# Spectral mixer with channel MLP, four layers: outer products added over two banks at once, weights' parts made beside the inner products

## The chip, the cores and the metric

The kernel runs on one core of a Trainium2 chip. Its engines run beside each other, each with its own queue in a fixed order: TensorE (PE in the profile, with its weight loads as PEld), VectorE (DVE), ScalarE (ACT), GpSimd (POOL) and SyncE (SP, whose queue issues all DMAs here). They wait for each other by semaphores. The metric is the device time of one execution in microseconds (us); the median of several runs counts.

## The reference

A token matrix x of 2048 x 576 goes through two pairs of layers, all in float32:

```python
x = x + _A_ref(_layernorm(x, axis=-1), A_dft_seq_re, A_dft_seq_im, A_dft_hid_re, A_dft_hid_im)
x = x + _B_ref(_layernorm(x, axis=-1), B_w1, B_b1, B_w2, B_b2)
x = x + _A_ref(_layernorm(x, axis=-1), A_dft_seq_re, A_dft_seq_im, A_dft_hid_re, A_dft_hid_im)
x = x + _B_ref(_layernorm(x, axis=-1), B_w1, B_b1, B_w2, B_b2)
```

`_A_ref` is the real part of a Fourier transform along the hidden dimension and along the sequence, as products with given cosine and sine matrices. `_B_ref` is a layer norm of its own, then `gelu(y @ w1 + b1) @ w2 + b2`, with w1 of 576 x 4608 and w2 of 4608 x 576.

## The kernel before

**Precision.** Each float32 operand of a product is split in two parts: the high part is the value rounded to TensorE's float32r format (a ScalarE copy), the low part is the rest (a subtraction). A product is then three matmuls, high x high, high x low and low x high (`PASSES`, L44). For w1 a block row of 288 values is held as two blocks of 128 and a third block in which the last 32 rows stand three times, so that high and low parts of the last rows share one matmul of 96 rows.

**Seven products for eight.** Each large product of 2 x 2 blocks is made by seven block products of sums and differences (Winograd's form of Strassen's scheme). They are numbered 1 to 7. `ORDER` (L33) is their order in the inner products, `OUTER` (L43) that in the outer products: 1, 6, 5, 3 and then 7, 4, 2.

**Stages.** For each layer pair: the sequence transform (`Sequence.run`), then for two halves of 1024 tokens the hidden transform (`hidden`) and the MLP (`mlp`). The four MLP stages are called passes 1 to 4 here. Pass 1 (layer 0, half 0; `first` is true) also makes the w2 parts and the rest of the w1 parts, and stores both to DRAM for the passes after it.

**One MLP pass.** F is cut in 18 pieces q; two of them, 2g and 2g + 1, make a group g (NG = 9). The loop at L1118 runs over g = 0 to 9. For g from 1 to 8 it does: the inner products of q = 2g (the *even inner phase*, seven products of seven matmuls with 512 columns), the outer products 1, 6, 5, 3 of group g - 1 (*outer phase A*, four products of 24 matmuls with 288 columns), the inner products of q = 2g + 1 (*odd inner phase*) and the outer products 7, 4, 2 of group g - 1 (*outer phase B*). g = 0 has inner phases alone, g = 9 outer phases alone.

*Inner phase* (`inner`, L976). Even q uses PSUM banks 0 to 3, odd q banks 4 to 7. Products 1 and 2 share the first of the four banks, 6 has the second, 5 and 3 share the third, 7 and 4 the fourth: the later product adds to what the earlier left, so it waits until that has been read. After product 1 ScalarE copies the bank (L1013), after 6 VectorE adds (L1015), after 5 ScalarE copies (L1019) and GpSimd adds the copy and product 1 and 6's sum (L1020), after 7 VectorE adds that (L1022), and product 4 may then write. Gelu follows in place (L986).

*Steps* (`step`, L1041). The result of an inner phase is turned into the seven left operands H of the outer products in eight steps: ScalarE copies the high part (L1047), VectorE or, from step 4 on, GpSimd makes the low part of the step before (L1051), and VectorE makes the next sum or difference from step 1 to 4. Steps are queued in `tasks`; `work(1)` puts one of them on the engines' queues, after each inner product and in each *slot* of an outer phase.

*Outer phase* (`outer`, L1070). A slot is half a product: 12 matmuls into the two banks of a pair `pp[2 * side + jj]`, six for each bank. After the matmuls of a slot come, in this order on the queues: a step, the second weights' work that is due (`advance`), a `tick`, and the addition of both banks to the accumulator in SBUF, one VectorE instruction for each bank (L1094, L1096). The slot after next writes the same pair. Phase A uses banks 4 to 7, phase B banks 0 to 3.

**Weights' parts.** `weights` (L244) is a generator for the w1 parts, 126 in number (18 pieces of seven). One pump of it takes the part begun before, makes its low part with two VectorE subtractions (L264, L265), stores it (L266), lets GpSimd make the next sum or difference of raw blocks where one is due, loads a raw block, and begins the next part with one ScalarE copy (L281). `tick(share)` pumps it in `share` of four calls: in three of four steps of the first sequence transform (L623), in one of four inner products and outer slots of pass 1 (L1031, L1088). `make` (L927) lists for a group of w2 when each of its seven parts is begun (`hi`, a ScalarE copy) and finished (`lo`, a VectorE subtraction and a store), when GpSimd makes sums of raw blocks, and when raw blocks of the next group are loaded. The first number of an entry is its due time: 0 to 6 are the products of the even inner phase, 7 to 14 the slots of phase A, 15 to 21 the odd inner phase, 22 to 27 phase B. The weights' loads for the inner and outer products (`load_w`) go over the same SyncE queue as these stores and loads. Buffers for w1 parts are five in pass 1 and seven in the others; those for w2 parts three.

## Time and profile before

| what | value |
|---|---|
| median of 3 runs | 2779.91 us |
| the runs | 2789.28, 2779.21, 2779.91 us |
| span of the profiled execution | 2780.2 us (no time of its own is listed for it) |
| mean granted TensorE clock | 0.996 |
| first matmul of the first sequence transform | 11.3 us |
| pass 1, from its first full inner phase to the end of its last | 472.7 to 875.3 us |
| pass 2, the same stretch | 1013.5 to 1379.1 us |
| pass 3, the same stretch | 1882.2 to 2247.9 us |
| pass 4, the same stretch | 2376.3 to 2741.9 us |

A row of busy time by stretches gives: the stretch, its length, then busy time and number of instructions of PE, PEld, DVE, ACT and POOL, the granted clock, the share of DMA time and GB/s. A row of the order of time gives: start, duration, engine, line, operation, output and inputs, number of instructions merged into it, and in brackets the idle time before it with what ended it. A row of the groups gives: line, engine, operation, shape and number, then busy time, mean duration in ns and idle time before. A row of waits gives: who waited for whom, us in total, times, longest.

### The profile page before, as it was taken

Reading aid. Unit: us, or ns where it says so; the run is one execution under the profiler, and the core shown is the slowest. Engines: PE = TensorE matmul, PEld = TensorE weight load, DVE = VectorE, ACT = ScalarE, POOL = GpSimd, SP = SyncE. Lnnn points to the kernel's source line nnn. Section 1 sums busy time; section 2 is a strip of 40 time slices with the busy share of each in tenths; the row PEclk is TensorE's granted clock in tenths of the full one; section 3 lists DMA queues with packets and bytes.
Section 4 is the critical chain, followed back from the end, with each engine's and each line's share of the span. In section 5 each row is a group of like instructions: output and inputs, shape, how many; then the busy total and the mean of one; then the engine's idle time right before and its main releaser. Section 6 shows DMA issues by size and latency. Waiting matters only on the chain. (4 is left out here: it accounts for less than half of the span.)

```text
span 2780.2 us, 46515 instructions
## 1 busy us (share of the span) xinstructions
PE 2687.9 (97%) x17596; PEld 2511.9 (90%) x17596; DVE 1793.9 (65%) x3179; ACT 1113.4 (40%) x1827; POOL 898.4 (32%) x836
## 2 busy tenths in 40 slices
PE   7999999999998999999989999999999999999999
PEld 7999998778887989898989999998888889988888
DVE  8888965777776555555577666555555564655555
ACT  6444434544443343333344333334333333433332
POOL 5232234544544442222241000043222234322223
PEclk9999999999999999999999999999999999999999
DMA  5676764777775646666563333426666664666664
GB/s 202 231 230 217 236 212 136 265 263 249 266 269 193 208 134 193 193 191 189 160 235 111 125 118 124 162 90 205 191 193 192 193 213 135 184 192 192 189 197 157
DMA packets 205551, 530.54 MB, mean 191 GB/s; under 512 B 21632, under 2 KB 56448, under 8 KB 205184
## 3 DMA queue, kind: packets, MB, share of 16 engines
q1 hardware_dynamic: 205328, 527.57, 59.2%
q8 instruction: 140, 2.29, 0.3%
q14 instruction: 83, 0.68, 0.1%
HBM read 420.73 MB, written 109.41 MB: 191 GB/s over the span
## 5 line engine op out<-in xcount | busy, mean ns | idle before, releaser
L198 PE MATMUL bank<-R 128*128 128x288 f32 (+2 forms) x16972 | 2629.2, 315 | 79.6 <-DVE A L188 42.6
L198 PEld LDWEIGHTS bank<-R 128*128 128x128 f32 x16972 | 2445.9, 189 | 253.8 <-DVE A L188 55.9
L188 DVE TENSOR_TENSOR A<-bank,A 128x288 f32<-128x288 f32 (+1 forms) x1260 | 561.6, 477 | 399.1 <-PE bank L198 356.6
L188 POOL TENSOR_TENSOR A<-A 128x512 f32<-128x512 f32 (+4 forms) x178 | 229.0, 1290 | 998.3 <-ACT A L1019 410.2
L191 POOL TENSOR_TENSOR R<-A,R 128x512 fp32r<-128x512 f32 x288 | 372.8, 1305 | 535.1 <-ACT R L1047 532.2
L191 DVE TENSOR_TENSOR R<-A,R 128x1024 fp32r<-128x1024 f32 (+6 forms) x575 | 475.6, 840 | 41.2 <-ACT R L544 25.0
L188 DVE TENSOR_TENSOR bank<-bank,A 128x512 f32<-128x512 f32 (+1 forms) x228 | 153.0, 671 | 360.1 <-POOL A L188 262.8
L1047 ACT ACTIVATE R<-A 128x512 fp32r<-128x512 f32 x288 | 175.6, 628 | 287.9 <-PE bank L198 256.6
L986 ACT ACTIVATE bank<-bank,b1t 128x512 f32<-128x512 f32 (+1 forms) x224 | 144.9, 647 | 359.6 <-DVE bank L188 198.1
L191 DVE TENSOR_TENSOR R<-bank,R 128x512 fp32r<-128x512 f32 (+4 forms) x408 | 251.4, 635 | 50.9 <-ACT R L194 44.5
L544 ACT ACTIVATE R<-A 128x1024 fp32r<-128x1024 f32 x196 | 204.1, 1054 | 147.4 <-DVE A L191 119.5
L191 POOL TENSOR_TENSOR A<-A 128x288 f32<-128x288 f32 (+2 forms) x170 | 211.1, 1251 | 151.5 <-DVE R L191 91.6
L191 DVE TENSOR_TENSOR A<-A 128x1024 f32<-128x1024 f32 (+2 forms) x116 | 130.5, 1130 | 4.2 <-ACT A L238 1.2
L1047 ACT ACTIVATE R<-bank 128x512 fp32r<-128x512 f32 x216 | 120.8, 596 | 29.3 <-PE bank L198 29.3
L194 ACT ACTIVATE R<-bank 128x512 fp32r<-128x512 f32 (+2 forms) x160 | 74.0, 514 | 145.8 <-PE bank L741 90.9
L1013 ACT ACTIVATE A<-bank 128x512 f32<-128x512 f32 (+1 forms) x76 | 43.7, 575 | 180.2 <-PE bank L198 171.0
L191 DVE TENSOR_TENSOR A<-bank,A 128x512 f32<-128x512 f32 x144 | 98.0, 681 | 0.1
L238 ACT ACTIVATE A<-A,moments 128x576 f32<-128x576 f32 x64 | 54.0, 868 | 107.6 <-POOL moments L221 75.8
L281 ACT ACTIVATE R<-A 128x384 fp32r<-128x384 f32 x126 | 65.1, 516 | 18.1 <-DMA w_parts<-R 7.4
L1019 ACT ACTIVATE A<-bank 128x512 f32<-128x512 f32 (+1 forms) x76 | 43.7, 575 | 62.4 <-PE bank L198 62.4
L584 DVE SCALAR_TENSOR_TENSOR A<-A 128x288 f32<-128x288 f32 x28 | 16.0, 571 | 77.4 <-POOL A L188 77.4
L219 POOL TENSOR_TENSOR moments<-moments,power 128x1 f32<-128x1 f32 x32 | 17.6, 551 | 144.1 <-DVE moments L216 144.1
(48 smaller groups left out, 670.9 us busy)
## 6 DMA issues: line engine op xcount, KB each, us to landing
R<-w_parts SPq DMA_DIRECT2D x504, 320.0 KB, 3.4
R<-w_parts SPq DMA_DIRECT2D x189, 576.0 KB, 3.7
A<-in_cs SPq DMA_DIRECT2D x112, 512.0 KB, 4.2
w_parts<-R SPq DMA_DIRECT2D x126, 320.0 KB, 3.3
w_parts<-R SPq DMA_DIRECT2D x63, 576.0 KB, 3.2
uv_mid<-A SPq DMA_DIRECT2D x32, 576.0 KB, 2.8
A<-in_w SPq DMA_DIRECT2D x72, 192.0 KB, 3.5
R<-dh_mid SPq DMA_DIRECT2D x36, 288.0 KB, 5.7
```

What stands on the lines that cost most here:

```text
L188: engine.tensor_tensor(dst, a, b, op=op)
L191: engine.tensor_tensor(dst, a, b, op=OP.subtract)
L194: nc.scalar.activation(hi, src, AF.Copy)
L198: nc.tensor.matmul(o, a, b, start=start, stop=stop, skip_group_check=True)
L219: nc.gpsimd.tensor_tensor(mv[:, 3:4], mv[:, 2:3], power[:, 0:1], op=OP.pow)
L238: nc.scalar.activation(dst, src, AF.Identity, bias=mv[:, 4:5], scale=mv[:, 3:4])
L281: nc.scalar.activation(at(n)[:, :3 * P], steps[n % 7][1], AF.Copy)
L544: nc.scalar.activation(self.cells[t, i](2, NP, P)[:, 0], self.source(t, i), AF.Copy)
L986: nc.scalar.activation(dst, src, AF.Gelu_apprx_tanh, bias=bias(f))
L1013: nc.scalar.activation(up, o, AF.Copy)
L1019: nc.scalar.activation(tp, o, AF.Copy)
L1047: nc.scalar.activation(H[q, k](2, TC)[:, 0], src, AF.Copy)
```

## The change

Five things are changed.

1. The eight PSUM banks are one tile, and a pair `pp[i]` is a view of two neighbouring banks. The addition of an outer slot, and that of a tile in the hidden transform, is one VectorE instruction over both banks (2 x 288) where there were two of 288.
2. The parts of w1 are laid out anew: low, high, shared, high, low. One VectorE subtraction of 3 x 128 makes all the low parts; for that the third block of the high part holds zeros outside rows 32 to 63 (a ScalarE instruction of its own with a scale for each partition, the new column `middle`), so that a part is begun with two ScalarE instructions. The raw blocks are laid out to fit, and so are the operands of the inner products.
3. `tick` is called in inner products alone, with a share of two of four, and its calls are spread evenly. In pass 1 that is seven pumps a group, as before.
4. `make` has new due times for all groups but the last: parts 1, 5 and 6 in the even inner phase, part 3 in phase A, parts 7, 4 and 2 in the odd inner phase. Both sums that follow part 1 are made at once.
5. Of three slots in an outer phase the third carries no step, except in the last two groups of outer products; the steps left over go to the next inner phase.

```diff
-    banks = [psum.tile([P, 512], F32, name=f"bank{i}") for i in range(8)]
-    pp = [(banks[2 * i], banks[2 * i + 1]) for i in range(4)]
+    bank = psum.tile([P, 8, 512], F32, name="bank")
+    banks = [bank[:, i] for i in range(8)]
+    pp = [bank[:, 2 * i:2 * i + 2] for i in range(4)]
...
+    middle = const.tile([P, 1], F32, name="middle")
...
+        def cut(a):
+            return a.rearrange("p (k f) -> p k f", f=P)
+
+        def high(n):
+            src, t = cut(steps[n % 7][1]), cut(at(n))
+            nc.scalar.activation(t[:, 1:4:2], src[:, 0:3:2], AF.Copy)
+            nc.scalar.activation(t[:, 2], src[:, 1], AF.Identity, bias=power[:, 2:3], scale=middle)
...
-            t = at(n)
-            sub(nc.vector, t[:, 3 * P:], src[:, :2 * P], t[:, :2 * P].bitcast(F32))
-            sub(nc.vector, t[32:64, 2 * P:3 * P], src[32:64, 2 * P:], t[32:64, 2 * P:3 * P].bitcast(F32))
-            dma(w1s[q, i - 1], t.bitcast(F32))
+            t = cut(at(n))
+            sub(nc.vector, t[:, 0:5:2], cut(src), t[:, 1:4].bitcast(F32))
+            dma(w1s[q, i - 1], at(n).bitcast(F32))
...
-                nc.scalar.activation(at(n)[:, :3 * P], steps[n % 7][1], AF.Copy)
+                high(n)
...
-        if ticks[0] % 4 < share:
+        if ticks[0] * share % 4 < share:
...
-            for e in range(2):
-                add(nc.vector, tile_x[:, e], o[e][:, :DH], tile_x[:, e])
+            add(nc.vector, tile_x, o[:, :, :DH], tile_x)
...
-            return [(1, lambda: hi(1, b11)),
-                    (2, lambda: (lo(1, b11), sub(pool, b11, b12, b11))), (3, lambda: sub(pool, x, b22, b11)),
-                    (5, lambda: hi(6, x)), (6, lambda: lo(6, x)),
-                    (7, lambda: hi(5, b11)), (8, lambda: (lo(5, b11), load_raw(g + 1, 0), sub(pool, x, b21, x))),
-                    (9, lambda: hi(3, b22)),
-                    (10, lambda: (lo(3, b22), sub(pool, b12, b22, b12), load_raw(g + 1, 2))),
-                    (12, lambda: hi(7, b12)), (13, lambda: (lo(7, b12), load_raw(g + 1, 1))),
-                    (14, lambda: hi(4, x)), (15, lambda: lo(4, x)),
-                    (16, lambda: hi(2, b21)), (17, lambda: (lo(2, b21), load_raw(g + 1, 3)))]
+            one = [lambda: hi(1, b11), lambda: (lo(1, b11), sub(pool, b11, b12, b11), sub(pool, x, b22, b11))]
+            six = [lambda: hi(6, x), lambda: (lo(6, x), sub(pool, x, b21, x))]
+            five = [lambda: hi(5, b11), lambda: (lo(5, b11), load_raw(g + 1, 0))]
+            three = [lambda: hi(3, b22), lambda: (lo(3, b22), sub(pool, b12, b22, b12), load_raw(g + 1, 2))]
+            seven = [lambda: hi(7, b12), lambda: (lo(7, b12), load_raw(g + 1, 1))]
+            four = [lambda: hi(4, x), lambda: lo(4, x)]
+            two = [lambda: hi(2, b21), lambda: (lo(2, b21), load_raw(g + 1, 3))]
+            if g == NG - 1:
+                return list(zip((1, 2, 5, 6, 7, 8, 9, 10, 12, 13, 14, 15, 16, 17),
+                                one + six + five + three + seven + four + two))
+            return list(zip((0, 1, 2, 3, 4, 5, 9, 10, 15, 16, 17, 18, 19, 20),
+                            one + five + six + three + seven + four + two))
...
-                    todo += [(w[:, k], yi[:, k]), (w[:, k], yi[:, 3 + k]), (w[:, 3 + k], yi[:, k])]
+                    todo += [(w[:, 1 + 2 * k], yi[:, k]), (w[:, 1 + 2 * k], yi[:, 3 + k]), (w[:, 4 * k], yi[:, k])]
...
-                    tick(1)
+                    tick(2)
...
+        slot = [0]
+
         def outer(g, i, side):
...
-                work(1)
+                work(slot[0] % 3 < 2 or g >= last - 1)
+                slot[0] += 1
                 advance()
-                tick(1)
...
-                for j in range(2):
-                    if i == 6 and g == 0:
-                        nc.vector.tensor_copy(to[:, j], o[j][:, :DH])
-                    else:
-                        add(nc.vector, to[:, j], o[j][:, :DH], to[:, j])
+                if i == 6 and g == 0:
+                    nc.vector.tensor_copy(to, o[:, :, :DH])
+                else:
+                    add(nc.vector, to, o[:, :, :DH], to)
...
+                    slot[0] = 0
                     for i in OUTER[f]:
                         outer(g - 1, i, 1 - f)
...
+    nc.gpsimd.memset(middle, 0.0)
+    nc.gpsimd.memset(middle[32:64], 1.0)
...
-                w1[:, :, at, k] = block[k * P:(k + 1) * P].transpose(1, 0, 2)
+                w1[:, :, at, 2 * k] = block[k * P:(k + 1) * P].transpose(1, 0, 2)
             for r in range(3):
-                w1[:, 32 * r:32 * r + 32, at, 2] = block[2 * P:].transpose(1, 0, 2)
+                w1[:, 32 * r:32 * r + 32, at, 1] = block[2 * P:].transpose(1, 0, 2)
```

On the engines' queues of the program that results, TensorE has the same instructions in the same order. In groups 2 to 7 of pass 1, GpSimd's queue now has in the even inner phase, in this order: two low parts of steps, the two sums that follow w2 part 1, a w1 sum, two low parts of steps, and then the sum after product 5 (L1020). VectorE has 662 instructions fewer, ScalarE 126 more.

More of the change, by code (lines that the diff above doesn't have):

```diff
@@ L739, in turn @@
             for k in range(KH):
-                at = (*a, *b)[k // 4][:, k % 4 * P:(k % 4 + 1) * P]
+                at = (a, b)[k // 8][:, k // 4 % 2, k % 4 * P:(k % 4 + 1) * P]
                 nc.tensor.transpose(at, v[:, k], ident)
-            for k0, k1, at in ((0, 4, a[0]), (4, 8, a[1]), (8, 9, b[0][:, 0:P])):
+            for k0, k1, at in ((0, 4, a[:, 0]), (4, 8, a[:, 1]), (8, 9, b[:, 0, 0:P])):
                 split(o[:, 0, k0:k1], o[:, 1, k0:k1], at.rearrange("p (k t) -> p k t", t=P))
@@ L806, in turn_y @@
                     o = space()
-                ob = o[i0 // 2 % 2]
+                ob = o[:, i0 // 2 % 2]
                 ni = min(2, 7 - i0)
@@ L817, in turn_y @@
             for i0 in (0, 4):
-                ob = o[i0 // 4]
+                ob = o[:, i0 // 4]
                 ni = min(4, 7 - i0)
@@ L846, in hidden @@
                     for e in range(2):
-                        mm(o[e][:, :DH], u(2, KH, P)[:, a, k], h.dd[k][b](2, DH)[:, e],
+                        mm(o[:, e, :DH], u(2, KH, P)[:, a, k], h.dd[k][b](2, DH)[:, e],
                            k == 0 and m == 0, k == KH - 1 and m == 2)
@@ L1078, in outer @@
                         for n, (a, b) in enumerate(PASSES):
-                            mm(o[j][:, :DH], h[:, a, at], w[:, b], i in (1, 5, 7, 2) and f == 0 and n == 0,
+                            mm(o[:, j, :DH], h[:, a, at], w[:, b], i in (1, 5, 7, 2) and f == 0 and n == 0,
                                i in (6, 3, 2, 4) and f == 1 and n == 2)
```

## The prediction

> **What bounds the kernel now.** I read the page first, then busy time by stretches, then the order of time in one group of the MLP.

> ```profile
> span 2780.2 us, 46515 instructions
> PE 2687.9 (97%) x17596; PEld 2511.9 (90%) x17596; DVE 1793.9 (65%) x3179; ACT 1113.4 (40%) x1827; POOL 898.4 (32%) x836
> ...
> 210.00:280.00 70.00, 70.00 (x532) 70.00 (x531) 62.03 (x83) 33.12 (x51) 19.73 (x12) 1.00 0.70 227
> ```

> TensorE sets the time: at 97% only some 90 us are idle, though a wait hidden in the modelled ends of its matmuls comes on top. The third row (busy time of PE, PEld, DVE, ACT, POOL; then clock and DMA) is a stretch of the sequence transform in which the first weights' parts are made: PE never pauses, so cheaper work on other engines gains nothing there. The MLP is where time can be had. The next rows cut one group (g = 3) of pass 1 (layer 0, half 0, which also makes the weights' parts) and one of pass 2, each into even inner phase, outer phase A (products 1, 6, 5, 3), odd inner phase and outer phase B (7, 4, 2). The cuts are where the first matmul of a phase starts.

> ```profile
> 588.02:599.30 11.28, 11.28 (x51) 9.24 (x50) 5.88 (x10) 5.02 (x9) 5.57 (x4) 1.00 0.82 256
> 599.30:615.87 16.57, 13.80 (x97) 12.92 (x96) 16.25 (x31) 7.59 (x15) 12.46 (x9) 1.00 0.72 248
> 615.87:627.81 11.94, 11.53 (x51) 9.16 (x50) 5.30 (x11) 4.60 (x8) 2.30 (x3) 1.00 1.00 352
> 627.81:638.01 10.20, 10.15 (x73) 9.66 (x72) 9.51 (x21) 5.26 (x11) 3.88 (x3) 1.00 0.50 179
> ...
> 1115.23:1126.53 11.30, 11.30 (x51) 9.24 (x50) 2.72 (x5) 3.51 (x6) 2.57 (x2) 1.00 0.73 203
> 1126.53:1139.97 13.44, 13.37 (x97) 12.90 (x96) 10.93 (x23) 4.58 (x9) 5.08 (x4) 1.00 0.56 179
> 1139.97:1151.26 11.29, 11.29 (x51) 9.24 (x50) 2.55 (x4) 3.20 (x5) 1.29 (x1) 1.00 0.72 201
> 1151.26:1160.83 9.57, 9.57 (x74) 9.56 (x73) 8.92 (x19) 4.50 (x9) 3.87 (x3) 1.00 0.60 189
> ```

> Phase B of pass 2 is bare: 72 matmuls in 9.57 us, 0.133 each, so bare A is 96 x 0.133 = 12.76, and a bare inner phase 11.29. A bare group is 2 x 11.29 + 12.76 + 9.57 = 44.9 us; pass 2 takes 45.6, pass 1 takes 49.99. In A of pass 1 DVE is busy 16.25 of 16.57 us: there VectorE is the limit, and 3.8 us are lost. Eight groups (g = 1 to 8) hold both kinds of phase, so pass 1 has 8 x 5.1 = 41 us to give and passes 2 to 4 some 0.7 a group.

> **The change part by part.** *Two-bank adds.* The 0.7 us of pass 2 are here:

> ```profile
> 1127.54 0.46 DVE L188 TENSOR_TENSOR A<-bank,A 128x288 f32<-128x288 f32 x1
> ...
> 1129.48 1.09 ACT L1047 ACTIVATE R<-bank 128x512 fp32r<-128x512 f32 x2 [0.84 <-PE bank L198]
> 1130.11 1.42 DVE L188 TENSOR_TENSOR A<-bank,A 128x512 f32<-128x512 f32 x3 [0.72 <-ACT R L1047]
> ...
> 1132.64 0.81 DVE L188 TENSOR_TENSOR A<-bank,A 128x288 f32<-128x288 f32 x2
> 1133.14 1.66 PEld L198 LDWEIGHTS bank<-R 128*128 128x128 f32 x12 [0.27 <-DVE A L188]
> ...
> 1135.07 5.09 PEld L198 LDWEIGHTS bank<-R 128*128 128x128 f32 x38 [0.27 <-DVE A L188]
> ```

> A slot is 12 matmuls, 1.59 us; it needs the bank pair that the slot before last filled, thus that slot's adds. Two adds take 0.81 (0.46 and, back to back, 0.35). For one of 2 x 288 there is no row: below, one add of 288 more elements at the 1.04 ns an element between 288 and 512 (0.46 and the 0.69 of a 512 add at 591.51, below) gives 0.76; above, no saving, 0.81. I take 0.76. What it saves is little, and it starts only when both banks are full, where the first of two adds now starts half a slot early. The larger part is the steps: of every three slots only two now carry a step, each step two DVE operations of 0.6 ahead of the add. So DVE needs about 1.9, 1.9 and 0.7 us in three slots of 4.8, and the later waits for an add go. One stays: in slot 1 the chain ACT (ends 1130.57), 0.6 us operation, merged add of 0.76 ends at 1131.5, or 4.97 into the phase, and slot 3 wants its banks at 4.78: 0.25 with the release. A in passes 2 to 4: 13.44 to 13.03. In B the add of slot 4 now follows a step and ends about when the next inner phase wants bank 0: +0.1. With g = 8, where every slot keeps its step and a merged add is later, I take -1.3 a pass, **-4 us** for three (ends -9, all of the 0.7 gone, and +3).

> *Outer phases of pass 1.* Out of A go two pumps of the weights' parts (the tick moves to every second inner product: seven a group as before) and the second and fourth pairs of second-weight parts (first what PE waited for from 475 to 885 us, then the group's DVE work by form):

> ```profile
> PE bank L198 <- DVE A L188: 20.4, 22, 1.8
> PE bank L198 <- DMA R<-w_parts: 3.3, 6, 0.8
> ```

> ```profile
> L191 DVE TENSOR_TENSOR R<-A,R 128x576 fp32r<-128x576 f32 x7 | 6.5, 923 | 0.0
> ...
> L191 DVE TENSOR_TENSOR R<-A,R 128x256 fp32r<-128x256 f32 x8 | 4.1, 508 | 0.0
> ...
> L281 ACT ACTIVATE R<-A 128x384 fp32r<-128x384 f32 x7 | 3.6, 517 | 0.0
> ...
> L191 DVE TENSOR_TENSOR R<-A,R 32x128 fp32r<-32x128 f32 x7 | 3.1, 442 | 0.1
> ```

> That is 2 x 0.92 + 2 x 0.95 = 3.7 us of DVE, one further step pair (1.2) goes to the inner phase's start, and the eight merged adds give 0.4: of 16.25 some 11 remain in 12.76, so PE bounds A again. What is left are the 0.25 as in pass 2 and two waits of 0.3 behind the part for product 3, still made here: 13.6, a gain of **3.0** (between 2.2 and 3.6). B loses its one or two pumps: 10.20 to 9.65, -0.55. The odd inner phase loses 0.65 (11.94 against 11.29) to weights that arrive late behind the queue's stores in A; these stores move away: -0.5.

> *One subtraction for two.* 0.508 + 0.442 becomes one of 384 elements, between the 0.508 of 256 and the 0.75 of 576 (at 570.03, below); I take 0.55. The 0.4 saved lies beside PE's work in the sequence transform, where PE has no pause, and in inner phases: nothing. Were PE not the limit there, it would be 0.4 a pump.

> *Where that work goes.* The even inner phase gets three parts instead of one or two, both GpSimd subtractions of the first part in its second product, three pumps instead of one or two, and the steps left over. What is late next is the GpSimd sum after product 5. Now it runs like this (the phase starts at 588.02):

> ```profile
> 591.51 0.69 DVE L188 TENSOR_TENSOR A<-bank,A 128x512 f32<-128x512 f32 x1 [2.06 <-PE bank L198]
> 592.12 2.51 DVE L191 TENSOR_TENSOR R<-A,R 128x576 fp32r<-128x576 f32 x3
> ...
> 592.94 1.54 POOL L191 TENSOR_TENSOR A<-A 128x576 f32<-128x576 f32 x1 [3.19 <-DVE R L191]
> ...
> 595.34 1.29 POOL L188 TENSOR_TENSOR A<-A 128x512 f32<-128x512 f32 x1 [0.86 <-ACT A L1019]
> ...
> 596.59 1.42 POOL L191 TENSOR_TENSOR A<-A 128x576 f32<-128x576 f32 x1
> 596.68 0.70 DVE L188 TENSOR_TENSOR bank<-bank,A 128x512 f32<-128x512 f32 x1 [2.06 <-POOL A L188]
> ```

> The sum ends at 596.63, 8.6 into the phase; DVE's add ends at 9.36; product 4, which adds into the bank that this add reads, starts at 6 x 1.61 = 9.67. The margin is 0.3 us. In the changed order GpSimd has, between the first part (DVE, 592.1 to 592.9, thus 4.85 into the phase) and this sum: two subtractions of 576 (in the old order one of them comes behind the sum), a weights' subtraction of 384 and two splits of 512. Nothing passes on an engine's queue.

> ```profile
> L191 POOL TENSOR_TENSOR R<-A,R 128x512 fp32r<-128x512 f32 x8 | 10.4, 1304 | 9.1 <-ACT R L1047 9.1
> ...
> L191 POOL TENSOR_TENSOR A<-A 128x576 f32<-128x576 f32 x4 | 6.3, 1587 | 3.2 <-DVE R L191 3.2
> ...
> L188 POOL TENSOR_TENSOR A<-A 128x384 f32<-128x384 f32 x1 | 1.0, 1020 | 3.7 <-ACT R L1047 3.7
> ```

> 4.85 + 2 x 1.5 + 1.05 + 2 x 1.3 = 11.5; the sum ends at 12.8, DVE at 13.6, product 4 starts at 13.8 instead of 9.67. That is **+4.2 us** in the even inner phase (3.8 with the shortest durations, 4.6 with the means). Such a delay is in the trace already, in group 1:

> ```profile
> 493.40 1.47 POOL L188 TENSOR_TENSOR A<-A 128x512 f32<-128x512 f32 x1
> ...
> 496.25 0.69 DVE L188 TENSOR_TENSOR bank<-bank,A 128x512 f32<-128x512 f32 x1
> ...
> 497.00 5.18 PEld L198 LDWEIGHTS bank<-R 128*128 128x128 f32 x32 [1.60 <-DVE bank L188]
> ```

> SyncE's queue is held too: the raw weights' load behind the third pump waits for a GpSimd operation that follows the sum, and the loads of the next phase's weights stand behind it. They go out near 14.5 us and are wanted after phase A: no cost. ScalarE's pump becomes two instructions for one of 0.517: between that and twice it; I take 0.8, and in the odd inner phase the copy of product 5 then comes 0.5 late against a margin of 0.3: +0.2. In passes 2 to 4 the left-over steps put four splits of 1.3 ahead of the sum, the first ready as the phase starts, so they end before product 5 does at 6.45: nothing.

> [...]

> ```profile
> 602.73 1.44 POOL L191 TENSOR_TENSOR A<-A 128x576 f32<-128x576 f32 x1
> ...
> 603.59 1.20 DVE L191 TENSOR_TENSOR R<-A,R 128x576 fp32r<-128x576 f32 x1
> 570.03 0.75 DVE L191 TENSOR_TENSOR R<-A,R 128x576 fp32r<-128x576 f32 x1
> ```

> DVE took 1.20 for 0.75, as GpSimd ended at 604.17. [...]

> *Sum.* A group of pass 1 now loses 4.2, gains 3.0 + 0.55 + 0.5 and loses 0.2: +0.35. Groups 2 to 7: +2. Group 8 has no pumps left, its chain is 1.05 shorter: -0.5. Group 1 has no splits in front of the sum and already has its stall: -4. Before group 1 the pumps double, where weights are late as it is: +1 (0 to +3). Merged adds of the hidden transform, 32 pairs at 0.05: -0.5. With the -4 of the other passes: 2780.2 - 6 = **2774 us**. The span stands 0.3 us above the median of the runs, which I leave out.

> **The rivals.** *Faster.* Phase A falls to 13.0 as in pass 2 (-0.6), the chain runs at its shortest (3.8, -0.4), and passes 2 to 4 get back all of the 0.7 (-9 for -4): -7 - 5 = -12, so 2762. For it speaks that DVE idles while PE stalls, and so enters A with nothing owed; against it, the count of GpSimd operations is fixed by the order.
> *Slower.* GpSimd's chain in the even inner phase is the new bound of the group, with every operation at the length it has beside VectorE (1.8, as the longest of 512 in the trace):

> ```profile
> 559.43 1.81 POOL L191 TENSOR_TENSOR R<-A,R 128x512 fp32r<-128x512 f32 x1
> ```

> Then 4.85 + 6 x 1.8 = 15.7, product 4 starts near 16.6, the stall is 6.9: +2.7 on seven groups, +19, so 2793; with the doubled pumps ahead of group 1 at their 3 us 2795. It decides once the stall passes 6.7 us. Against it: DVE has little to do while PE waits.
> *The steps gain nothing.* If A in pass 1 waits for its split parts and not for DVE, it stays near 15.5 and the group loses 1.9 more: 7 x 1.9 = +13, so 2787. The 16.25 of 16.57 speak against it.

> **How the numbers follow.** Forecast, with its own range 2766 to 2787: 0.48, to which the third rival adds 0.06. Faster rival 0.28; slower rival 0.18. A measurement of this kernel tells 0.5%, 13.9 us, from no change: the lines are 2766 and 2793.8. Range 2757 to 2797.

> **What would show it.** Right: PE waits of about 4 us for "DVE bank L190" in even inner phases 2 to 7 of pass 1, with the GpSimd sum starting some 11.5 us into the phase; A there 13 to 14 us and near 13.0 in passes 2 to 4; one add of 2 x 288 near 0.76; a pass-1 group at about 50 us. Wrong: the sum before 10 us, A over 15 us, or PE pausing in the sequence transform.

## The result, and the profile after

| kernel | median | runs | profiled run, span |
|---|---|---|---|
| before | 2780.76 us | 2789.28, 2779.21, 2779.91, 2781.61 | span 2780.2 |
| changed | 2813.46 us | 4, from 2812.36 to 2813.99 | 2813.99, span 2812.2 |

Ratio 1.0111, 95% interval 1.0095 to 1.0127: the change costs 32.7 us, where 6 us less was forecast.

The page of the changed kernel, busy time by engine:

```profile
span 2812.2 us, 45668 instructions
PE 2702.0 (96%) x17596; PEld 2525.1 (90%) x17596; DVE 1721.6 (61%) x2517; ACT 1145.9 (41%) x1953; POOL 887.2 (32%) x838
```

VectorE has 72 us less to do (1793.9 before), as the change meant. PE's busy time rose by 14 us (2687.9 before) with the same number of matmuls: some of them ran slower. Both are seen in busy time by stretches for one group (g = 4) of pass 1, cut where each phase's first matmul starts, and for A of pass 2 (columns as before: PE, PEld, DVE, ACT, POOL, granted clock, DMA share, GB/s):

```profile
646.52:664.13 17.61, 13.07 (x51) 10.31 (x50) 8.28 (x11) 7.95 (x16) 11.40 (x9) 0.87 0.65 210
664.13:678.67 14.54, 14.43 (x97) 13.85 (x96) 10.67 (x16) 5.36 (x9) 7.27 (x6) 0.92 0.53 191
678.67:691.10 12.43, 11.52 (x52) 9.16 (x50) 6.23 (x10) 6.90 (x14) 1.71 (x2) 1.00 0.74 236
691.10:700.62 9.52, 9.52 (x74) 9.47 (x72) 8.25 (x13) 4.21 (x8) 3.60 (x3) 1.00 0.97 382
...
1204.52:1217.58 13.06, 13.03 (x97) 12.80 (x96) 10.06 (x15) 4.80 (x9) 4.65 (x4) 1.00 0.53 181
```

Means over groups 2 to 7, before and after: even inner phase 11.28 to 17.61, A 16.60 to 14.35, odd inner 11.69 to 12.42, B 10.19 to 9.54. A group pays 6.33 + 0.73 and gets 2.25 + 0.65: +4.16 us, six times. With +1.5 for group 1, +3.9 for group 8, +3.05 for the last outer products and -1.5 ahead of them this is the 31.8 us by which pass 1 ends later; passes 2 to 4 give 0.4 in each A, and what lies between them loses as much.

The even inner phase in order of time, GpSimd's and VectorE's rows and the matmuls that wait:

```profile
650.71 1.22 DVE L193 TENSOR_TENSOR R<-A,R 128x576 fp32r<-128x576 f32 x2
651.54 4.67 POOL L193 TENSOR_TENSOR A<-A 128x576 f32<-128x576 f32 x3 [5.53 <-DVE R L193]
...
653.96 2.67 DVE L193 TENSOR_TENSOR R<-A,R 128x576 fp32r<-128x576 f32 x2 [2.03 <-ACT R L941]
...
656.18 2.79 POOL L193 TENSOR_TENSOR R<-A,R 128x512 fp32r<-128x512 f32 x2
...
658.93 1.26 POOL L190 TENSOR_TENSOR A<-A 128x512 f32<-128x512 f32 x1
...
660.23 1.30 DVE L190 TENSOR_TENSOR bank<-bank,A 128x512 f32<-128x512 f32 x2 [3.59 <-POOL A L190]
```

GpSimd never idles from 651.54 to the sum behind product 5, which starts at 658.93, 12.4 us into the phase. VectorE's add follows, and product 4 starts at 660.98, 14.46 into the phase; bare, it would at 9.67. That is a pause of 4.8 us, and in the table of waits it is what TensorE waited for most, ten times up to 4.5 us, in the stretch from 471 to 951 us:

```profile
PE bank L200 <- DVE bank L190: 34.3, 10, 4.5
```

The prediction did not price what comes behind the pause. Stretches of 3.41 us around it, and product 4 by itself:

```profile
656.18:659.60 3.42, 0.27 (x2) 0.00 (x0) 0.45 (x1) 0.00 (x0) 3.42 (x4) 1.00 0.96 297
659.60:663.01 3.41, 2.03 (x5) 1.66 (x6) 2.42 (x4) 1.95 (x4) 2.30 (x3) 0.50 0.53 179
663.01:666.42 3.41, 3.41 (x14) 3.13 (x13) 0.70 (x1) 1.18 (x2) 3.24 (x3) 0.50 0.94 301
666.42:669.83 3.41, 3.41 (x28) 3.41 (x26) 2.49 (x4) 1.66 (x3) 0.00 (x0) 1.00 0.89 347
660.98:664.13 3.15, 3.15 (x7) 2.51 (x8) 1.67 (x3) 1.93 (x4) 2.04 (x3) 0.50 0.68 187
```

After a stretch in which PE did nearly nothing the granted clock is 0.50 for two such stretches (in group 6 for one), then 1.00 again: 14 matmuls in the third row against 28 in the fourth, and product 4's seven take 3.15 us where a bare product takes 1.61. So of the 6.33 us a group, 4.8 are the pause and 1.5 the clock; the rest of the half-speed time falls into A.

### The profile page after: what moved, and what is told of

Same layout as the page of the kernel before. It is cut to its first block, busy times and chain, and to the rows that moved or that the text cites. A ratio compares the mean times of both kernels' runs of the same rounds, so it can differ in the third digit from the quotient of the medians.

```text
span 2812.2 us, 45668 instructions
## 1 busy us (share of the span) xinstructions
PE 2702.0 (96%) x17596; PEld 2525.1 (90%) x17596; DVE 1721.6 (61%) x2517; ACT 1145.9 (41%) x1953; POOL 887.2 (32%) x838
## 4 chain that ended last, share of the span: by engine, by line
PE 70%; DVE 4%; DMA 3%; issue 2%; POOL 2%; ACT 1%; SPq 0%; DVEq 0%; POOLq 0%; ACTq 0%
PE bank L200 70%; DVE R L193 2%; DMA R<-w_parts 1%; DVE A L190 1%; DMA R<-dh_mid 1%; POOL A L193 1%; PE bank L750 1%; POOL R L193 1%; DMA A<-in_cs 0%; POOL A L190 0%; DMA A<-x_mid 0%; DVE bank L190 0%; DVE moments L215 0%; DVE A L193 0%; DVE moments L230 0%
## 5 line engine op out<-in xcount | busy, mean ns | idle before, releaser
L190 DVE TENSOR_TENSOR A<-bank,A 128x576 f32<-128x576 f32 (+3 forms) x732 | 517.5, 715 | 469.1 <-PE bank L200 387.8
L190 POOL TENSOR_TENSOR A<-A 128x576 f32<-128x576 f32 (+4 forms) x178 | 230.0, 1295 | 908.1 <-ACT A L591 350.2
L193 DVE TENSOR_TENSOR R<-A,R 128x1024 fp32r<-128x1024 f32 (+4 forms) x449 | 438.2, 1004 | 61.3 <-ACT R L941 25.8
L190 DVE TENSOR_TENSOR bank<-bank,A 128x512 f32<-128x512 f32 (+1 forms) x228 | 152.2, 671 | 355.4 <-POOL A L190 256.6
L193 POOL TENSOR_TENSOR A<-A 128x288 f32<-128x288 f32 (+2 forms) x170 | 197.0, 1170 | 154.4 <-DVE R L193 84.1
L221 POOL TENSOR_TENSOR moments<-moments,power 128x1 f32<-128x1 f32 x32 | 17.6, 551 | 147.9 <-DVE moments L218 147.9
L997 ACT ACTIVATE A<-bank,b1t 128x512 f32<-128x512 f32 (+1 forms) x76 | 50.4, 663 | 29.4 <-DVE bank L190 29.2
```

What stands on the lines that cost most here:

```text
L190: engine.tensor_tensor(dst, a, b, op=op)
L193: engine.tensor_tensor(dst, a, b, op=OP.subtract)
L997: nc.scalar.activation(dst, src, AF.Gelu_apprx_tanh, bias=bias(f))
```

## The experiments

Eighteen kernels, e1 to e18. Each ratio is against runs of the kernel before on the same chip (their medians: 2780.76 us beside the changed kernel, 2783.69 to 2785.20 beside e1 to e18), with its 95% interval. Phases are means over groups 2 to 7 of pass 1 in the profiled run; "late A" is the median of A over groups 2 to 7 of passes 2 to 4.

| run | us | ratio | even | A | odd | B | late A |
|---|---|---|---|---|---|---|---|
| before | | 1 | 11.28 | 16.60 | 11.69 | 10.19 | 13.44 |
| changed | 2813.46 | 1.0111 (1.0095-1.0127) | 17.61 | 14.35 | 12.42 | 9.54 | 13.03 |
| e1 | 2796.34 | 1.0039 (1.0024-1.0054) | 15.05 | 13.91 | 12.88 | 9.59 | 13.06 |
| e2 | 2801.26 | 1.0059 (1.0044-1.0074) | 16.23 | 13.56 | 12.31 | 9.56 | 13.04 |
| e3 | 2796.85 | 1.0045 (1.0028-1.0062) | 15.54 | 13.90 | 12.59 | 9.54 | 13.04 |
| e4 | 2776.35 | 0.9968 (0.9955-0.9981) | 12.22 | 14.52 | 11.75 | 9.96 | 13.03 |
| e5 | 2794.03 | 1.0035 (1.0023-1.0046) | 12.72 | 15.43 | 12.65 | 10.18 | 13.43 |
| e6 | 2809.85 | 1.0090 (1.0075-1.0105) | 14.13 | 14.58 | 12.44 | 9.90 | 13.58 |
| e7 | 2805.82 | 1.0079 (1.0064-1.0094) | 11.29 | 17.06 | 11.78 | 10.67 | 13.58 |
| e8 | 2782.51 | 0.9993 (0.9983-1.0002) | 12.29 | 14.50 | 12.51 | 9.55 | 13.06 |
| e9 | 2803.79 | 1.0071 (1.0056-1.0086) | 17.38 | 14.93 | 12.54 | 9.55 | 12.76 |
| e10 | 2767.66 | 0.9941 (0.9926-0.9955) | 12.21 | 15.48 | 11.84 | 9.57 | 12.76 |
| e11 | 2772.83 | 0.9964 (0.9950-0.9979) | 12.20 | 13.51 | 14.62 | 9.55 | 12.83 |
| e12 | 2763.81 | 0.9929 (0.9914-0.9944) | 12.20 | 13.12 | 14.64 | 9.55 | 12.74 |
| e13 | 2801.67 | 1.0067 (1.0051-1.0084) | 15.82 | 14.49 | 12.64 | 9.82 | 13.03 |
| e14 | 2772.67 | 0.9955 (0.9940-0.9969) | 11.62 | 16.33 | 12.34 | 9.55 | 12.76 |
| e15 | 2747.28 | 0.9866 (0.9851-0.9880) | 11.67 | 13.92 | 12.43 | 9.55 | 12.74 |
| e16 | 2751.20 | 0.9880 (0.9865-0.9895) | 12.32 | 13.93 | 12.61 | 9.55 | 12.74 |
| e17 | 2779.00 | 0.9978 (0.9969-0.9987) | 11.29 | 16.17 | 12.26 | 9.89 | 13.44 |
| e18 | 2782.43 | 0.9990 (0.9981-1.0000) | 11.28 | 17.64 | 11.76 | 9.78 | 13.41 |

### The pause and the clock (e1 to e4, from the changed kernel)

e1, the sum on VectorE:

```diff
-                    add(nc.gpsimd, tp, tp, up)
+                    add(nc.vector if first else nc.gpsimd, tp, tp, up)
```

> The changed kernel, but the sum behind product 5 is made by VectorE in pass 1 (0.7 us there) instead of GpSimd, so that it no longer queues behind GpSimd's two subtractions, the weights' subtraction and two splits. Main theory (all of the loss is the pause that this queue makes in front of product 4, and what the clock does after the pause): even inner phases of pass 1 fall from 17.6 us to 11.4-12.2, phase A from 14.5 to 13.2-13.8, no matmul of 512 columns takes 427 ns in groups 2 to 7, and the whole kernel comes to 2750-2768 us, faster than both. Rival (the doubled pumps and the parts pushed into the even inner phase overload ScalarE or VectorE whoever makes the sum): the even inner phase stays over 14 us and the time over 2790. Rival (two-bank adds or the spread steps cost by themselves): even inner phases fall, but the time stays above the 2781 of the kernel before.

The time fell by 0.7% and not to where the theory had it; even inner phases stay at 15.1 us. The order of time in group 4 shows why:

```profile
650.75 0.83 DVE L190 TENSOR_TENSOR A<-A 128x512 f32<-128x512 f32 x1 [2.52 <-ACT A L1030]
...
651.50 3.11 DVE L193 TENSOR_TENSOR R<-A,R 128x576 fp32r<-128x576 f32 x2
652.42 3.31 POOL L193 TENSOR_TENSOR R<-A,R 128x512 fp32r<-128x512 f32 x2
...
654.53 1.28 DVE L190 TENSOR_TENSOR bank<-bank,A 128x512 f32<-128x512 f32 x2
```

The sum is now done at 651.58, but on VectorE's queue two part subtractions (576 and 384 elements) stand between it and the add that frees product 4's bank; beside GpSimd's work the two took 3.11 us (0.75 + 0.55 alone in the changed kernel), and GpSimd's two splits beside them 3.31 for 2.6. So the theory "GpSimd's queue alone" falls: the parts moved into the even inner phase hold both queues. The pause is 2.9 us (matmul start to matmul start), and five of the six groups still have the half clock.

e2, 12 extra matmuls in front of product 4, results unused:

```diff
+                if first and i == 4 and q % 2 == 0 and q > 1:
+                    for _ in range(12):
+                        mm(banks[6], w[:, 1], yi[:, 0], True, True)
```

> The changed kernel with 12 extra matmuls of 512 columns ahead of product 4 in every even inner phase of pass 1 from the second on; their result is never used. They fill 12 x 0.23 = 2.8 us of the 4.9 us in which TensorE waits, and shorten nothing. [...] Rival (matmuls behind the pause are slow because VectorE, ScalarE and GpSimd come together in PSUM and SBUF there): they stay at 427 ns and the time is 2813 or more.

```profile
640.63:655.15 14.52, 12.94 (x56) 9.98 (x54) 6.60 (x9) 6.02 (x13) 9.44 (x7) 1.00 0.63 215
655.15:656.88 1.73, 1.73 (x8) 1.43 (x9) 1.67 (x3) 1.73 (x4) 0.62 (x2) 1.00 0.27 47
```

Product 4 comes 14.52 us into the phase as it did (14.46), and then takes 1.73 us at a granted clock of 1.00 for 3.15 at 0.50; A falls to 13.56. Useless work in the pause saves 0.5%: the slow matmuls were the clock.

e3, the second GpSimd sum behind part 1 one product later, so behind the sum after product 5:

```diff
-lambda: (lo(1, b11), sub(pool, b11, b12, b11), sub(pool, x, b22, b11))]
+lambda: (lo(1, b11), sub(pool, b11, b12, b11))]
+rest = [lambda: sub(pool, x, b22, b11)]
```

> The changed kernel with one of the two GpSimd subtractions behind part 1 (x = b22 - b11) moved one product later, so that by program order it follows the sum behind product 5, as in the kernel before. [...] If the clock stays up in most groups, 2785; if it halves as before, 2800. Rival (GpSimd is not what the sum waits for): no change, 2813.

The rival did not come: the pauses fell from 4.9 to 3.3-3.45 us (matmul start to matmul start), four of the six were followed by a clock of 0.5 and two were not, and the time lies between the two cases.

e4, `make` with its old list, all else changed:

```diff
-            return list(zip((0, 1, 2, 3, 4, 5, 9, 10, 15, 16, 17, 18, 19, 20),
-                            one + five + six + three + seven + four + two))
+            return [(1, lambda: hi(1, b11)),
+                    (2, lambda: (lo(1, b11), sub(pool, b11, b12, b11))), (3, lambda: sub(pool, x, b22, b11)),
...
```

> The changed kernel with the old order and the old due slots of the second weights' parts (the change of this list undone; two-bank adds, one subtraction, pumps in inner products and spread steps stay). Main theory: the queue ahead of the sum is one subtraction shorter and the parts are back in phase A: even inner phase 12-15 us, phase A 13.5-15.5, time 2772-2790. Rival (the pumps in inner products make the pause): the even inner phase stays over 16 us and the time over 2800.

Even inner phases of groups 2 to 7 take 12.2 us, with no pause over 1.1 and no half clock behind them, and the kernel is 0.3% faster than before. Undoing the due times alone takes back 1.4%, the most of all single undoings here.

### Single edits and their undoing (e5 to e9)

e5, the kernel before with the new list of `make` alone (the diff of e4 the other way round):

> The kernel before with one thing of the change: the new order and due slots of the second weights' parts. Theory (queue): GpSimd gets one subtraction of 576 elements (1.5 us) more in front of the sum behind product 5, against 0.86 us in which it now idles there; VectorE gets two part subtractions more between product 5 and product 7. Product 4 starts 0.7-1.5 us late, the clock stays up, even inner phases of pass 1 take 12.0-12.8 us, phase A falls from 16.57 to 14.0-15.0, and the time to 2764-2775: the new due times alone gain, and the loss needs the pumps and the left-over splits beside them. Rival (the due times alone make the pause): even inner phases over 15 us, time 2800 or more.

The even inner phase came as expected, 12.7, with a pause of 1.55 us (matmul start to matmul start) and no half clock behind it; the gain did not come. A fell by 1.2 us and not by 2, and the odd inner phase, to which three parts moved, grew by 1.0. The due times lose by themselves, a third of a per cent.

e6, the changed kernel without the spreading:

```diff
-                work(slot[0] % 3 < 2 or g >= last - 1)
+                work(1)
```

> The changed kernel, but every slot of an outer phase keeps its step, so that all eight are done in phase A. Theory (queue): two GpSimd splits (2.7 us) leave the queue in front of the sum; the pause falls from 4.9 to 1.8-2.5 us and the clock stays up; even inner phases of pass 1 12.9-13.8 us, phase A there 13.5-14.5 (1.2 us of VectorE come back), phase A of passes 2 to 4 13.1-13.4 instead of 13.03; time 2775-2790. Rival (VectorE's part subtractions between products 5 and 7 decide by themselves): the pause stays over 3.5 us and the time over 2800.

The two splits left the queue, and the pause fell to 2.5 us as expected; yet the time hardly moved (the intervals touch). Busy time by stretches in group 4 shows the clock at 0.51 behind a pause of 2.5 us, as in two of the six groups:

```profile
649.25:652.66 3.41, 1.32 (x7) 0.78 (x5) 2.26 (x4) 0.57 (x2) 3.41 (x3) 0.99 1.00 343
652.66:656.07 3.41, 3.41 (x9) 2.73 (x10) 1.69 (x4) 1.91 (x4) 2.30 (x3) 0.51 0.85 237
```

And late A rose to 13.6, over the 13.44 of before, and late B to 9.90 from 9.56. That second loss is the merged add, which e7 shows by itself.

e7, the kernel before with two-bank adds alone (the change's hunks for `banks`, `pp` and the adds):

```diff
-                    for j in range(2):
-                        add(nc.vector, to[:, j], o[j][:, :DH], to[:, j])
+                    add(nc.vector, to, o[:, :, :DH], to)
```

> The kernel before with one thing of the change: outer products' adds over two banks at once. Theory: 0.05 us an add, and it starts later for the first bank; phase A of passes 2 to 4 stays within 13.2-13.5 us, so the fall to 13.03 is the spreading's; phase A of pass 1 16.2-16.6; time 2775-2782. Rival (the merged add alone brings the 0.4 us a phase): A of passes 2 to 4 at 13.0-13.1, time 2768-2775. Rival (two banks of one tile make matmuls and adds wait for each other): A over 13.5, time over 2785.

A clear loss, 0.8%, in every phase with outer products: +0.5 in A and B of pass 1, +0.14 in late A, +0.33 in late B, +2.6 in the long stretch from the last outer products of pass 2 to the end of the second sequence transform (409.7 to 412.4 us; 1.8 of it lie in the stretch's first 240 matmuls, the outer products). The order of time in B of pass 2, first of the kernel before (phase from 1151.26):

```profile
1158.49 0.81 DVE L188 TENSOR_TENSOR A<-bank,A 128x288 f32<-128x288 f32 x2
```

and with merged adds (phase from 1209.47):

```profile
1216.86 0.75 DVE L189 TENSOR_TENSOR A<-bank,A 128x576 f32<-128x576 f32 x1
...
1217.67 1.88 PEld L199 LDWEIGHTS bank<-R 128*128 128x128 f32 x14 [0.23 <-DVE A L189]
```

The last of six slots starts at 5/6 of 9.56 = 7.97 in a bare phase. Of two adds the first is done at 7.23 + 0.46 = 7.69 and frees the bank that the slot writes first; the second bank is wanted half a slot later. The merged add starts at 7.39 and frees both at 8.14: TensorE waits. It saves VectorE 0.06 us and lengthens the time to the first bank by 0.3. The numbers of the second rival came too (A over 13.5 us, time over 2785), but not by its reason: with the banks in one tile and separate adds (e9) late A is 12.76, as with separate tiles (e14), so the one tile costs nothing here.

e8, the changed kernel with parts 1 and 6 at the old due times, 5 and 3 in A, 7, 4 and 2 in the odd inner phase:

```diff
-            return list(zip((0, 1, 2, 3, 4, 5, 9, 10, 15, 16, 17, 18, 19, 20),
-                            one + five + six + three + seven + four + two))
+            return list(zip((1, 2, 3, 5, 6, 7, 8, 9, 10, 15, 16, 17, 18, 19, 20),
+                            first + six + five + three + seven + four + two))
```

(`first` is `one` with its second GpSimd subtraction as an entry of its own.)

> The changed kernel with another placing of the second weights' parts: those for products 1 and 6 at the old slots with the old order of GpSimd's subtractions, 5 and 3 in phase A, only 7, 4 and 2 moved into the odd inner phase. Theory (the loss is what stands in front of the sum; VectorE has room in A for two parts): even inner phases of pass 1 as with the old due times, 12.0-12.4 us, phase A 13.3-14.0, odd inner 11.5-12.6, B 9.6; a group 47-48 us against 50.0 before; time 2755-2768, faster than both. Rival (A stays near 14.5 for another reason): 2768-2776.

The rival came: A stays at 14.5 us though two parts have left it. In its order of time a part subtraction of 1.20 us stands in front of a merged add, and TensorE waits 1.1 us for that add. So not VectorE's sum but its order sets A. No gain over before.

e9, the changed kernel with two adds of one bank (in the hidden transform too):

```diff
-                    add(nc.vector, to, o[:, :, :DH], to)
+                    add(nc.vector, to[:, j], o[:, j, :DH], to[:, j])
```

> The changed kernel with two adds of one bank each again, everything else as changed. Theory (a merged add frees the first of its two banks later, which alone cost 0.3 to 0.5 us a waiting outer phase and 2.6 us in the hidden transform; the spread steps hide most of it): phase A of passes 2 to 4 12.8-13.0 us instead of 13.03, the hidden transform 2-3 us shorter, time 2800-2811. Rival (behind spread steps the merged add is free or gains): A of passes 2 to 4 13.03-13.2, time 2811-2818.

Late A is 12.76, bare: the spreading alone is worth 0.67 a phase, and the merged add takes 0.26 of it back. In the changed kernel the merged adds cost 0.4%.

### Old due times, and the order in a slot (e10 to e12)

e10 is e4 with the diff of e9; e11 is e4 with the (merged) add of a slot ahead of `work` and `advance`; e12 has both.

```diff
+                to = goal[i][:, 2 * jj:2 * jj + 2]
+                add(nc.vector, to, o[:, :, :DH], to)
                 clock[0] += 1
                 work(slot[0] % 3 < 2 or g >= last - 1)
                 slot[0] += 1
                 advance()
-                to = goal[i][:, 2 * jj:2 * jj + 2]
-                add(nc.vector, to, o[:, :, :DH], to)
```

> The changed kernel with the old due times of the second weights' parts and two adds of one bank each. Theory (merged adds free the first bank late): phase A of pass 1 14.0-14.4 us instead of 14.5, B 9.6-9.9 instead of 9.6-10.4, the rest as with old due times alone; time 2762-2772. Rival: 2775-2780, as with merged adds.

> The changed kernel with the old due times, and in each outer slot the (merged) add issued ahead of the slot's step and part, not behind them. Theory (in A of pass 1 it is VectorE's order that is late: a step and a part of 1.2 us stand in front of the add that frees the banks, while VectorE has idle time later in the phase): A 13.0-13.6 us instead of 14.5, B 9.6; time 2758-2768. Rival (A waits for VectorE's sum of work whatever its order): A 14.2-14.6, time 2772-2780.

> As the run with old due times and the add ahead of step and part, with two adds of one bank each. Theory (late first bank): 2-6 us under that run, 2754-2766, the gain in the hidden transform and in A of passes 2 to 4 (12.8-12.9). Rival (with the add first the merged add costs nothing): within 2 us of that run.

e10 has the time that was expected, by another way: A of pass 1 got longer (15.5), all the gain over e4 is in B, in the stretch with the second sequence transform (2.4 us, 1.7 of them in the outer products at its start) and in passes 2 to 4. So in A of pass 1 merging gained 1.0 us a phase; why, these runs do not show. e11 and e12 bring A to 13.5 and 13.1, so order was the reason; but the odd inner phase then takes 14.6, so e11 misses its time, and the order gains nothing clear (the intervals of e11 and e4 overlap, and so do those of e12 and e10). Separate adds take 9 us off e11, more than expected. Two stretches of e12, and its waits between 540 and 836 us:

```profile
652.21:665.29 13.08, 13.08 (x97) 12.79 (x96) 12.51 (x26) 7.31 (x14) 7.88 (x7) 1.00 0.91 319
665.29:678.99 13.70, 11.52 (x52) 9.16 (x51) 6.76 (x11) 6.61 (x13) 2.58 (x3) 1.00 0.90 312
```

```profile
PE bank L200 <- DMA R<-w_parts: 14.0, 6, 2.8
PE bank L200 <- DVE bank L190: 3.9, 6, 0.6
```

Waits for VectorE's accumulator adds are gone (16.1 us in that window of the kernel before), and six waits for the weights of an inner product have come, 14.0 us in all: DMA is busy 0.9 through A and the odd inner phase. What VectorE no longer holds up, late weights do. Whether they are late by the load on the DMA engines or by the order of SyncE's queue, where the loads stand behind stores that wait for VectorE's parts, is not told apart.

### What was still open (e13 to e18)

e13, the changed kernel with the old ticks:

```diff
-                    tick(2)
+                    tick(1)
...
                 advance()
+                tick(1)
```

> The changed kernel with the old ticks: a pump at every fourth slot of inner and outer phases alike, not at every second inner product. Theory (queue): one weights' subtraction (1.0 us) and what it holds up leave the queue in front of the sum, so the pause is 3.3-4.0 us and the clock still halves in most groups; even inner phases of pass 1 15.0-16.6 us, phase A 14.3-15.2, odd inner 11.6-12.2; time 2795-2808. Rival (the pumps are the main thing): even inner under 14 us, time under 2790. Rival (they cost nothing): 2811-2816.

As expected: without the pumps in the queue the pause is 3.7 us, equal in all six groups, and five of them have the half clock behind it. The pumps' move makes 0.4%.

e14, the kernel before with the spreading alone:

```diff
-                work(1)
+                work(slot[0] % 3 < 2 or g >= last - 1)
+                slot[0] += 1
```

> The kernel before with one thing of the change: a step in two of three slots of an outer phase. Theory: phase A of passes 2 to 4 falls from 13.44 to 12.77 as in the changed kernel with separate adds, -12 us; in pass 1 two splits (2.7 us) now stand in front of the sum behind product 5, against 0.86 us of idle time there, so even inner phases take 12.0-13.2 us and phase A 15.2-16.2; time 2764-2776. Rival (the splits end before product 5 does): even inner stays at 11.3, time 2755-2764.

A gain of 0.45%, most of it late A at 12.76. In pass 1 the even inner phase loses 0.3 us, less than expected.

e15 is e12 with the old ticks (the diff of e13); e16 is e15 with the sum on VectorE in pass 1 (the diff of e1).

> The run with old due times, add first and separate adds, with the old ticks too. Theory (the odd inner phase waits 2 us for weights because its stores, the pumps' 320 KB among them, crowd the queue and the DMA engines): odd inner 11.6-12.6 us instead of 14.6, even inner 11.3-12.0, phase A 13.1-13.8, time 2742-2756. Rival (the crowding is the sum of bytes, wherever they are stored): odd inner stays over 13.5 us or A grows by as much, time 2758-2768.

> As the run before, with the sum behind product 5 on VectorE in pass 1. Theory (what is left in the even inner phase is GpSimd's queue): even inner phases 11.3-11.5 us, 3-6 us under the run before. Rival (VectorE's queue makes it as late): no change or slower.

e15 is the best of all, 2747.28 us, 1.3% faster than before. Group 4, four phases:

```profile
626.18:637.87 11.69, 11.57 (x52) 9.16 (x50) 5.67 (x11) 5.90 (x11) 7.61 (x6) 1.00 0.78 249
637.87:651.77 13.90, 13.41 (x97) 12.86 (x96) 13.70 (x28) 7.89 (x17) 5.13 (x4) 1.00 0.88 306
651.77:664.07 12.30, 11.78 (x51) 9.07 (x50) 7.79 (x10) 5.77 (x11) 9.13 (x7) 1.00 0.87 308
664.07:673.59 9.52, 9.52 (x73) 9.52 (x72) 8.22 (x18) 4.80 (x10) 2.78 (x3) 1.00 0.57 219
```

A group takes 47.6 us in the mean for 49.8; the odd inner phase gave back 2.2 of its 3 us when the pumps' stores went back to the outer phases (A paid 0.8). e15 differs from e14 by the add ahead of the step, the one subtraction and the one tile, apart from the ticks' spacing in the first sequence transform, and is 0.9% faster; the subtraction alone is worth 0.2% (e17), so by difference most of this is the order in the slot. e16's theory fell: with the sum off GpSimd the even inner phase got longer (12.3): on VectorE's queue a weights' subtraction of 384 elements stands behind the sum and ahead of the add, and between 471 and 870 us TensorE waited eight times for VectorE's adds to a bank, 6.8 us in all (e15: twice, 1.2 us). The times of the two kernels are not told apart.

e17 and e18, the kernel before with the one subtraction alone, and with pumps in inner products alone (the change's hunks for each; their core):

```diff
-            sub(nc.vector, t[:, 3 * P:], src[:, :2 * P], t[:, :2 * P].bitcast(F32))
-            sub(nc.vector, t[32:64, 2 * P:3 * P], src[32:64, 2 * P:], t[32:64, 2 * P:3 * P].bitcast(F32))
+            sub(nc.vector, t[:, 0:5:2], cut(src), t[:, 1:4].bitcast(F32))
```

```diff
-        if ticks[0] % 4 < share:
+        if ticks[0] * share % 4 < share:
...
-                    tick(1)
+                    tick(2)
...
-                tick(1)
```

> The kernel before with one thing of the change: the first weights' parts by one subtraction (and two ScalarE instructions instead of one). Theory: VectorE saves 0.4 us a pump, in front of the MLP (some 1 us at its start) and in phase A of pass 1, where VectorE is the limit and a pump or two are made (0.4-0.8 us a group); time 2770-2781. Rival (the second ScalarE instruction makes copies in inner phases late): inner phases longer by 0.5 us or more, time 2785-2795.

> The kernel before with one thing of the change: pumps at every second inner product, none in outer phases. Theory (queue): one weights' subtraction of 1.0 us more ahead of the sum against 0.86 us of idle time, so even inner phases 11.3-12.0 us; phase A 14.9-15.8 us instead of 16.6, B 9.6; odd inner 12.0-12.8; time 2768-2778. Rival (the pumps make a pause by themselves): even inner over 13 us, time over 2785.

The one subtraction gains 0.2%, in A, B and at the start of pass 1; the odd inner phase loses 0.6 us a group. The pumps' move does nothing that can be told: the even inner phase hides them as expected, but A got longer in place of shorter, 18.1 us in four groups and 16.6 and 16.9 in two. Two stretches of A in group 4, one of the four:

```profile
663.04:666.45 3.41, 1.65 (x13) 1.41 (x12) 3.41 (x6) 0.00 (x0) 1.00 (x1) 1.00 0.55 207
666.45:669.86 3.41, 3.41 (x16) 3.41 (x16) 2.73 (x5) 2.30 (x4) 2.68 (x2) 0.50 0.51 153
```

VectorE is busy throughout the first, PE waits 1.8 us for its add, and the second runs at half clock. In the two groups without it A is what it was before: the two pumps taken out of A gave nothing, as its waits are for VectorE's order.

Added up, the edits done alone make +0.35 - 0.45 + 0.79 - 0.22 - 0.10 = +0.37%, some 10 us. Together they make 1.11%. The other 20 us exist only where the edits meet: in the even inner phase, whose delays alone are 1.4 (due times), 0.3 (spreading) and nothing (the others), and together 6.3.

## Why the prediction was wrong

- *The sum's start and the pause.* The mechanism, the place and the order of the queue were right; the pause was 4.8 us where 4.2 was taken (4.6 with the means). Start 5.02 for 4.85, the three subtractions 4.67 for 4.05, two splits 2.79 for 2.6. VectorE's two operations beside them took 2.67 for the 1.3 they take alone (0.75 + 0.55): beside each other the operations of both engines ran longer, which the 4.2 us of the sum do not include.
- *What follows a pause.* This is the step that failed. The sum priced the pause as a shift of product 4 and of nothing else. The clock made product 4 dearer by 1.5 us and A by 0.8 (14.35 against 13.56 in e2, which keeps the clock): 2.3 of the 3.8 us by which a group missed its +0.35. Half of PE's busy time in the stretches at 0.50 behind these pauses, 1.4 to 3.0 us a pause in groups 1 to 8, makes 17.9 us. Without them the time would be near 2795.5, an estimate from that sum, and so at the upper end of the range: the clock carried it out, and the terms below had used up the room. The trace of before had such a case, in its last outer products, and the prediction does not use it:

```profile
899.30:902.73 3.43, 1.38 (x10) 1.38 (x11) 1.49 (x3) 0.68 (x1) 0.00 (x0) 1.00 1.03 398
902.73:906.14 3.41, 0.75 (x4) 0.40 (x2) 0.71 (x2) 1.39 (x3) 0.00 (x0) 0.50 1.03 413
```

- *A of pass 1.* Forecast 13.6, and 13.56 where the clock stays up. Right, though its reason was half wrong: e8 and e11 show that the order on VectorE's queue, not its sum of work, sets this phase in the changed kernel, and in e18 two pumps less leave it as long or longer.
- *The odd inner phase.* -0.3 forecast, +0.73 measured: 1.0 of the 3.8. The stores' going from A was taken as a gain; the three parts that arrive were taken as free. With the parts elsewhere and the same pumps (e4) the phase takes 11.75, with them 12.4 to 12.5 (changed, e8). Before, the wait lay ahead of product 3, in four of the six groups; now product 4 starts 0.8 to 1.7 us late in all six, three times for weights and three times for VectorE.
- *Merged adds.* 0.76 us was the duration forecast and measured (0.75 to 0.76). A at 13.03 in passes 2 to 4 was right in its number and its place: one wait is left, ahead of slot 3, where a merged add ends 4.94 us into the phase (4.97 forecast). What the prediction did not say is that this wait is the merging's own price: the spreading gives 0.67, and the add takes 0.26 back (e9 has no such wait). It counted merged adds as gains of 0.05 each, also in pass 1 and in the hidden transform, and alone they cost 0.8% (e7). The three passes gave 4.7 us where 4 were forecast, but the stretches between them lose as much, which the sum did not have (1.6 in the one with the second sequence transform, 1.3 of it in the outer products at its start).
- *One subtraction, ScalarE's pair.* 0.55 us as taken, and 0.41 + 0.48 for the 0.8 taken. The 0.4 us was put at nothing; alone it gains 0.2% (e17).
- *Group 1 and the end.* -4 forecast, +1.5 measured: its stretch of inner products grew by 5.4 us with a pause of 3.2 and the half clock behind it. Group 8 was to give 0.5 and cost 3.9: its even inner phase took 16.0 us, with a pause of 3.3 and the half clock. The last outer products (+3.05) were not in the sum.
- *The rivals.* The slower one named the right mechanism, GpSimd's chain as the new bound of the group, with a stall of 6.9 us that decides once it passes 6.7. The pause stayed below that and cost as much, since the clock doubled the price of what followed. It got 0.18 where it should have had the most. The faster rival and the third (A near 15.5) did not come.

## What to carry to other kernels

A pause of TensorE can cost more than its length: add what runs behind it at half clock, up to 3.0 us here (half of the 5.92 us that PE was busy in the two stretches at 0.50 from 714.21 us of the changed kernel). Waits from 1.8 us (e18) up had it in some groups. Before work is moved off a busy engine, list for each in-order queue what will stand ahead of the one instruction that frees the next bank; issue that instruction first, and the rest of the slot after it. Here this paid only once the weights came in time again (e15, not e11). And an add over two buffers frees both late: look first who waits for the first of them.

## What the runs showed of the hardware

```profile
714.21:717.62 3.41, 1.65 (x13) 1.61 (x13) 3.41 (x7) 0.26 (x1) 0.76 (x1) 1.00 0.45 169
717.62:721.03 3.41, 3.41 (x27) 3.41 (x26) 3.18 (x7) 2.04 (x4) 2.96 (x2) 1.00 0.49 153
```

The traces of the kernel before and of the changed one, each cut on its grid, without their first 20 us and last 8 us, have 15 stretches at full clock with one at half clock behind them, and PE was busy in these for at most 0.48 of the stretch; of the other 1579 none was busy for less than 0.45. The two stretches that set these bounds are in the kernel before, 1.63 us busy and then the half clock, 1.53 and then the full one, each with the stretch behind it:

```profile
2268.06:2271.47 3.41, 1.63 (x13) 1.39 (x12) 1.49 (x3) 0.93 (x2) 0.00 (x0) 1.00 1.03 412
2271.47:2274.89 3.42, 3.42 (x16) 3.42 (x16) 2.90 (x7) 1.80 (x3) 0.00 (x0) 0.50 1.03 402
...
1407.90:1411.32 3.42, 1.53 (x12) 1.29 (x10) 3.42 (x5) 0.00 (x0) 1.29 (x1) 1.00 0.97 314
1411.32:1414.73 3.41, 0.00 (x0) 0.00 (x0) 3.41 (x7) 1.06 (x1) 2.20 (x3) 1.00 1.00 369
```

In these two traces the clock came back only behind stretches at half clock in which PE was busy for 0.83 or more, and stayed at 0.50 behind those of at most 0.73. These are traces that happened to have such stretches; no run varied the share by itself.

VectorE's subtractions of 576 elements in pass 1 of the changed kernel took from 0.75 us, with GpSimd idle (650.71), to 1.84 beside it (522.07), and GpSimd's two splits in e1 took 3.31 us beside VectorE for 2.6. In three of these subtractions 0.44 us were left of GpSimd's running instruction when VectorE's began and made 1.06 (885.63), 0.76 made 1.38 (653.96) and 1.23 made 1.84 (522.07), so each ended 0.61 to 0.62 us after the other. With the sum moved from GpSimd to VectorE (e1) VectorE's two part subtractions still took 3.11 us beside GpSimd for 1.3.
